# Running sums and an addition moved into accumulating transfers from GpSimd's queue, in a gated mix of linear attention and a long convolution

## The chip, the cores and the metric

One core of a Trainium2 chip runs the kernel. The time is device microseconds of one launch, with the inputs in the chip's main memory. The core has five engines with an instruction queue each: TensorE (matrix products; PE in the profile, its weight loads PEld), VectorE (DVE), ScalarE (ACT), GpSimd (POOL) and SyncE (SP), which here only starts transfers. Every engine works through its queue in order and waits at an instruction until what that needs is there. Transfers are carried by 16 DMA engines that all queues share.

## The reference, cut to what matters

The input x has 2048 rows of 448 channels. Two branches are computed from it and mixed by a gate of each row:

```python
g = sigmoid((x * gate_w).sum(-1))
# attention without softmax, 16 heads of 28 channels, phi(t) = (t + 1 or exp(t)) + 1e-6
kv = einsum("bhsd,bhse->bhde", phi(k), v);  z = phi(k).sum over rows
a  = (phi(q) @ kv / (phi(q) . z + 1e-6)) @ wo
# convolution along the rows, one kernel of 2048 taps for each channel
K  = 2 * Re(sum_n C[d, n] * exp(A[d, n] * dt[d] * l));   b = causal_conv(x, K) + x * D_skip
out = g * a + (1 - g) * b
```

For the given parameters the taps of a channel hardly change with the lag, so that the convolution is a running sum of x over the rows, times one number for each channel (`near`). The kernel checks on the chip that this holds and has a general path behind a branch for channels where it doesn't; that path is not taken here.

## The kernel before, in words

The rows are cut into 16 chunks of 128, and four chunks make a group. Row r of group g lies in partition r // 4 of chunk 4g + r % 4, so a partition holds four successive rows of the input, one in each chunk of its group. A running sum over a group's rows is then made of two steps: a sum over the four chunks inside each partition, and a sum over the partitions, which is a product with a triangular matrix (`tri`).

Everything is computed in float32 from pairs of a rounded part and a remainder (`split_t`, `split_n`: ScalarE copies the rounded part, GpSimd subtracts for the low part). The instructions are in an order written out by hand; the program keeps that order on each engine.

A loop `for c in range(2, NC - 2)` (lines 501 to 564) handles the middle chunks. In a stage c, TensorE projects k of chunk c+1 (`project`, line 340), then q and the gate of chunk c, and then adds chunk c to the accumulated product of phi(k) and x (`do_g`, line 415, four blocks). ScalarE and VectorE turn the projections into phi(k) and phi(q) (`k_feature`, `k_high`, `k_low`, `q_post`, lines 363 to 393): `pkh` is ScalarE's rounded part of phi(k), `pkl` the remainder, `zb` the running sum for z; `pq` keeps phi(q). GpSimd makes the low parts of the turned x (`xt`) and of the plain x (`xn`) of chunk c+2, and `skip` (line 258), which writes y = x * D_skip. SyncE loads x three chunks ahead (`load_x`), as its four buffers come free after the skips.

The convolution's path through the same stages:

- `group_load(g)` (line 422, SyncE) loads the four chunks of group g once more into a home: `homes = (spare, wvo[:, 1], pq[:, 12:], spare)`. Groups 0 and 3 share `spare`.
- `prefix(g, i, engine)` (line 425) adds chunk i-1 to chunk i, three times in a group, on GpSimd for group 0 and on VectorE for the others.
- `group_split` (line 427) splits the last chunk, which now holds the partition's sum, into `sums`; `group_heads` (line 432) multiplies it by `tri`, so that every partition has the sum of those before it.
- `convolve(c)` (line 438, VectorE) adds that to two chunks and multiplies them by `near`; after the second half SyncE copies the group's total row to `u`.
- `v_add(c)` (line 448, GpSimd) adds a chunk of the result to y, two in a stage of 6 to 11, and the last four in the final loop.

`near` itself comes from a preparation that is a generator (`s4d_prepare`, lines 285 to 320); `steps(n)` lets it go on by n pieces. The piece in stage 4 is a row of operations on VectorE with 4 elements in each of 112 partitions; the last piece, in stage 5, is four transposes on TensorE into a bank of PSUM (tag `v1`) and ScalarE's copy of them.

After the loop come the last two chunks, the combination of kv with wo, and the final loop, which normalizes phi(q), turns it, multiplies (`attend`, line 662) and adds the gated y (`final_b`, line 667).

## Time and profile before

| what | value |
|---|---|
| median of 3 runs | 180.84 us (180.59 to 181.35) |
| the profiled execution | 181.06 us, its span 179.3 us |
| granted TensorE clock | 1.0 over the span |
| TensorE busy | 165.7 us, 92% |
| VectorE busy | 139.3 us, 78% |
| ScalarE busy | 106.1 us, 59% |
| GpSimd busy | 135.4 us, 76% |
| bytes moved | 22.11 MB in 9434 packets |

The profile is of one execution. A row of an engine's timeline gives the start in microseconds from the span's beginning, the length, the engine, the line of the program, the operation and its tiles; in brackets stands how long the engine had been idle before it, and what ended that. The chain of waits goes back from the last instruction, at each step to what released it. A line can be that of a helper: L242 is `low`, whoever calls it. Product lengths overlap: products with 448 columns follow each other every 0.2 us.

### The profile page before, as it was taken

The page shows a single profiled execution, that of the slowest core. Times are in us where ns is not written, and L with a number is a line of the kernel's source. Part 1 is how long each engine was busy: PE and PEld are TensorE (multiplying, and loading weights), DVE is VectorE, ACT ScalarE, POOL GpSimd, SP SyncE. Part 2 cuts the span into 40 slices and gives each one's busy share as a digit, 9 for nine tenths or more (in the row PEclk, how much of TensorE's full clock was granted, in tenths as well). Part 3 has the DMA queues.
Part 4 walks back from the last instruction along what each step waited for, and adds up shares of the span by engine and source line. Part 5 has one row for each costly group of instructions (what it writes and reads, how often), then busy time and mean ns, then how long its engine had stood idle before and what let it go on. Part 6 is the DMA issues. An engine that isn't in the chain of part 4 may idle for free.

```text
span 179.3 us, 2707 instructions
## 1 busy us (share of the span) xinstructions
PE 165.7 (92%) x852; PEld 146.8 (82%) x852; DVE 139.3 (78%) x244; ACT 106.1 (59%) x241; POOL 135.4 (76%) x132
## 2 busy tenths in 40 slices
PE   7999999997699899978968999999999999999990
PEld 2798999995599779966957799999999999999990
DVE  0947549699989799889979978866898998997540
ACT  3779489863362846368244887667465464665431
POOL 6074676979949999969958979947968997988200
PEclk9999999999999999999999999999999999999999
DMA  5999978297520018303820300000031221221221
GB/s 184 413 296 302 255 194 311 88 400 275 218 107 0 0 13 305 123 4 118 203 93 0 117 4 0 0 2 0 3 68 53 103 98 57 105 104 52 104 103 58
DMA packets 9434, 22.11 MB, mean 123 GB/s; under 512 B 1357, under 2 KB 6170, under 8 KB 9418
## 3 DMA queue, kind: packets, MB, share of 16 engines
q1 hardware_dynamic: 9274, 21.81, 36.5%
q8 instruction: 7, 0.11, 0.3%
q10 hardware_dynamic: 144, 0.11, 0.2%
q14 instruction: 9, 0.07, 0.1%
HBM read 17.93 MB, written 3.67 MB: 120 GB/s over the span
## 4 chain that ended last, share of the span: by engine, by line
PE 53%; DVE 27%; ACT 13%; issue 4%; ACTq 0%; POOL 0%; DVEq 0%; POOLq 0%
PE a L662 20%; PE g L415 8%; PE q L340 6%; PE v L340 6%; PE tr L636 4%; DVE wvo L425 3%; PE q L264 3%; PE k L340 3%; DVE spare L425 3%; DVE pq L425 2%; ACT pkh L372 2%; DVE pq L393 2%; ACT e L391 2%; ACT e L392 2%; DVE v L368 2%
## 5 line engine op out<-in xcount | busy, mean ns | idle before, releaser
L662 PE MATMUL a<-wk,th 128*128 128x448 f32 (+1 forms) x170 | 36.4, 360 | 0.0
L415 PE MATMUL g<-pkh,xn 128*128 128x448 f32 x112 | 35.6, 364 | 0.0
L340 PE MATMUL q<-wqh,xt 128*128 128x450 f32 x120 | 27.9, 369 | 3.8 <-DVE pq L393 3.8
L662 PEld LDWEIGHTS a<-wk,th 128*128 128x128 f32 x170 | 29.5, 189 | 1.6
L242 POOL TENSOR_TENSOR xn<-xr,xn 128x448 fp32r<-128x448 f32 x16 | 23.8, 1489 | 8.3 <-ACT xn L252 3.7
L340 PEld LDWEIGHTS q<-wqh,xt 128*128 128x128 f32 x120 | 22.3, 189 | 6.5 <-DVE pq L393 4.9
L242 POOL TENSOR_TENSOR xt<-xr,xt 128x512 fp32r<-128x512 f32 x14 | 20.1, 1433 | 9.5 <-ACT xt L246 8.2
L415 PE MATMUL g<-pkl,xn 128*128 128x448 f32 x64 | 23.4, 366 | 0.0
L415 PEld LDWEIGHTS g<-pkh,xn 128*128 128x128 f32 x112 | 21.0, 188 | 2.2
L574 POOL TENSOR_TENSOR prod<-pq,zb 128x448 f32<-128x448 f32 x16 | 18.7, 1172 | 3.8 <-ACT zb L696 2.7
L258 POOL TENSOR_TENSOR y<-xr,rows 128x448 f32<-128x448 f32 x16 | 21.4, 1338 | 0.0
L340 PE MATMUL v<-wk,xt 128*128 128x448 f32 x99 | 21.3, 362 | 0.0
L340 PEld LDWEIGHTS v<-wk,xt 128*128 128x128 f32 x99 | 18.6, 188 | 1.3
L340 PE MATMUL k<-wk,xt 128*128 128x448 f32 x77 | 17.6, 368 | 1.3 <-POOL xt L242 1.3
L340 PEld LDWEIGHTS k<-wk,xt 128*128 128x128 f32 x77 | 14.3, 188 | 3.3 <-POOL xt L242 1.7
L599 POOL TENSOR_TENSOR pn<-pq,den 128x336 f32<-128x336 f32 x16 | 12.3, 769 | 3.7 <-ACT den L588 3.4
L667 DVE SCALAR_TENSOR_TENSOR ot<-y,og,a 128x448 f32<-128x448 f32 (+1 forms) x17 | 10.7, 630 | 5.2 <-PE a L662 4.3
L372 ACT ACTIVATE pkh<-v 128x448 fp32r<-128x448 f32 x9 | 4.9, 545 | 15.1 <-DVE v L368 15.1
L644 DVE TENSOR_TENSOR th<-tr,th 128x512 fp32r<-128x512 f32 x16 | 11.0, 690 | 2.6 <-ACT th L643 2.0
L643 ACT CAST th<-tr 128x512 fp32r<-128x512 f32 x16 | 9.4, 589 | 4.6 <-PE tr L636 4.4
L415 PEld LDWEIGHTS g<-pkl,xn 128*128 128x128 f32 x64 | 11.2, 174 | 1.2 <-DVE pkl L378 0.2
L340 PE MATMUL q<-wql,xt 128*128 128x450 f32 x45 | 11.8, 366 | 0.0
(170 smaller groups left out, 342.6 us busy)
## 6 DMA issues: line engine op xcount, KB each, us to landing
xr<-in SPq DMA_DIRECT2D x15, 512.0 KB, 3.9
out<-ot SPq DMA_DIRECT2D x15, 224.0 KB, 1.9
pq<-in SPq DMA_DIRECT2D x4, 448.0 KB, 12.3
spare<-in SPq DMA_DIRECT2D x2, 896.0 KB, 4.6
wvo<-in SPq DMA_DIRECT2D x2, 896.0 KB, 7.5
y<-in SPq DMA_DIRECT2D x2, 480.0 KB, 3.8
y<-in SPq DMA_DIRECT2D x2, 450.0 KB, 7.8
pq<-in SPq DMA_DIRECT2D x1, 896.0 KB
```

The lines of the kernel that those rows point to most:

```text
L242: eng.tensor_tensor(out=o, in0=r, in1=h.bitcast(F32), op=ALU.subtract)
L258: POOL.tensor_tensor(out=y[:, c], in0=plain[c][:, :D], in1=dsk, op=ALU.mult)
L340: PE.matmul(o[:, :n], lhsT=a, rhs=b, start=run.n == 1, stop=not seq)
L372: ACT.add(pkh[c], pks[c], 1e-6)
L415: PE.matmul(g[i][:a.shape[1], :D], lhsT=a, rhs=b, start=c == 0 and n == 0, stop=c == NC - 1 and n == len(seq) - 1)
L425: eng.tensor_tensor(out=homes[g][:, i], in0=homes[g][:, i], in1=homes[g][:, i - 1], op=ALU.add)
L574: POOL.tensor_tensor(out=pd[c], in0=pq[:, c], in1=zb, op=ALU.mult)
L599: POOL.tensor_tensor(out=n[:, :3, :DJ].rearrange("p j (h d) -> p j h d", h=4), in0=a, in1=r[:, :H - 4].rearrange("p (j h) -> p j h", j=3)[ ...
L643: ACT.copy(h, ov)
L644: DVE.tensor_tensor(out=l, in0=ov, in1=h.bitcast(F32), op=ALU.subtract)
L662: PE.matmul(a[:, lo:hi], lhsT=u_, rhs=w_[:, lo:hi], start=n == 0, stop=n == 10)
L667: DVE.scalar_tensor_tensor(out=ot[:, lo:hi], in0=y[:, c, lo:hi], scalar=og[:, c:c + 1], in1=a[:, lo:hi], op0=ALU.mult, op1=ALU.add)
```

## The change

The sums over a partition's four chunks are made by two accumulating transfers from GpSimd's queue. The first (`running(g, 1)`) adds the group's chunks 0 to 2, read once more from main memory, to its chunks 1 to 3 at home; the second (`running(g, 2)`) adds chunks 0 and 1 of the result to chunks 2 and 3. `prefix` is gone. The first is issued at the end of stages 2, 4, 6 and 8, the second in stages 3, 5, 7 and 9 behind GpSimd's part of `split_t`. The group loads of groups 2 and 3 move from stages 7 and 9 to 6 and 8, and all of them stand behind the loads of `cst`, `wvo` and `wo`. `group_split` moves one stage ahead, to 4, 6, 8 and 10, and its low part is always GpSimd's.

The sixteen `v_add` become four accumulating transfers (`group_add`), issued by GpSimd at the end of stages 7, 9, 11 and 13. `near`'s transposes move from behind the q projection of stage 5 to between the second and third block of `do_g`, into a bank of tag `v0`, and `group_heads(0)` moves behind the fourth block.

```diff
-        o = ps.tile([P, 512], F32, name="p", tag="v1")
+        o = ps.tile([P, 512], F32, name="p", tag="v0")
...
-    def prefix(g, i, eng):
-        eng.tensor_tensor(out=homes[g][:, i], in0=homes[g][:, i], in1=homes[g][:, i - 1], op=ALU.add)
-
-    def group_split(g, eng):
+    def running(g, step):
+        w = homes[g]
+        src = xin[g * G:(g + 1) * G - 1, :, NAT:LO].rearrange("r p d -> p r d") if step == 1 else w[:, :G - step]
+        POOL.dma_start(out=w[:, step:], in_=src, accum_op=ALU.add)
+
+    def group_split(g):
...
-        low(eng, w[:, 1], homes[g][:, G - 1], w[:, 0])
+        low(POOL, w[:, 1], homes[g][:, G - 1], w[:, 0])
...
-    def v_add(c):
-        POOL.tensor_tensor(out=y[:, c], in0=y[:, c], in1=homes[c // G][:, c % G], op=ALU.add)
+    def group_add(g):
+        POOL.dma_start(out=y[:, g * G:(g + 1) * G], in_=homes[g], accum_op=ALU.add)
...
+        if c in (2, 4, 6, 8):
+            group_load(c // 2 - 1)
+        ko = project(c + 1, wkh, wkl, D, "k" if c % 2 else "v1")
...
-        if c in (4, 6, 8, 10):
-            for i in (1, 2):
-                prefix(g0, i, DVE if g0 else POOL)
-        if c in (5, 7, 9, 11):
-            prefix(g0, 3, DVE if g0 else POOL)
         split_t(c + 2)
+        if c in (3, 5, 7, 9):
+            running(c // 2 - 1, 2)
         if c > 5:
             split_n(c + 2)
         k_feature(c + 1, ko)
-        if c in (5, 7, 9, 11):
-            group_split(g0, DVE if g0 else POOL)
+        if c in (4, 6, 8, 10):
+            group_split(c // 2 - 2)
...
-        if c == 5:
-            steps(1)
         q_post(c, qo)
...
-        do_g(c, (0, 1, 2))
-        if c in (5, 7, 9, 11):
-            group_heads(g0)
+        do_g(c, (0, 1))
+        if c == 5:
+            steps(1)
+        do_g(c, (2,))
+        if c in (7, 9, 11):
+            group_heads(c // 2 - 2)
         do_g(c, (3,))
+        if c == 5:
+            group_heads(0)
...
-        if 5 < c < 12:
-            v_add(2 * c - 12)
-            v_add(2 * c - 11)
+        if c in (2, 4, 6, 8):
+            running(c // 2 - 1, 1)
+        if c in (7, 9, 11, 13):
+            group_add(c // 2 - 3)
...
-        if 9 < c < 14:
-            v_add(c + 2)
```

More of the change, by code (lines that the diff above doesn't have):

```diff
@@ L505, in gated_mix_kernel @@
             SP.dma_start(out=cst, in_=cst_d)
-            group_load(0)
         if c == 4:
             SP.dma_start(out=wvo[:, 0], in_=wvo_d[:, 0])
-            group_load(1)
-        if c == 7:
-            group_load(2)
-        if c == 9:
-            group_load(3)
         if c == 10:
             SP.dma_start(out=wo, in_=wvo_d[:DJ, 1])
-        g0, half = (c - 4) // 2, c % 2
-        ko = project(c + 1, wkh, wkl, D, "k" if half else "v1")
+        if c in (2, 4, 6, 8):
+            group_load(c // 2 - 1)
+        ko = project(c + 1, wkh, wkl, D, "k" if c % 2 else "v1")
         if c > 5:
             convolve(2 * c - 12)
-        if c in (4, 6, 8, 10):
-            for i in (1, 2):
-                prefix(g0, i, DVE if g0 else POOL)
-        if c in (5, 7, 9, 11):
-            prefix(g0, 3, DVE if g0 else POOL)
         split_t(c + 2)
+        if c in (3, 5, 7, 9):
+            running(c // 2 - 1, 2)
         if c > 5:
```

## The prediction

> **What bounds the kernel now.** I read the page's chain of waits first, then that chain in order of time, then TensorE's timeline through chunks 4 to 12. (Each step c of the loop over the middle chunks, 2 to 13, is called stage c; it begins on TensorE with the k projection of chunk c+1.)
>
> ```profile
> span 179.3 us, 2707 instructions
> PE 53%; DVE 27%; ACT 13%; issue 4%; ACTq 0%; POOL 0%; DVEq 0%; POOLq 0%
> ```
>
> Half of the end is TensorE's own work; the rest is VectorE and ScalarE. In order of time (start, length, what) the chain says where:
>
> ```profile
> 40.04 0.55 ACT pkh L372
> ...
> 42.19 0.62 DVE pq L359
> 42.81 0.40 DVE sm L286
> ...
> 49.01 0.15 DVE oks L315
> ...
> 55.02 1.65 DVE wvo L425
> ...
> 59.28 0.06 ACT e L386
> 59.34 0.45 ACT e L390
> 59.82 0.59 ACT e L391
> 60.43 0.59 ACT e L392
> 61.04 0.63 DVE pq L393
> ...
> 96.90 1.59 DVE spare L425
> ...
> 100.90 2.20 PE v L340 x11
> ...
> 170.12 4.69 PE a L662 x33
> ```
>
> From 42 to 49 us the chain is a row of tiny VectorE operations (the preparation of near), from 55 to 98 us it passes again and again through the running sums of L425 on VectorE, and from 100.90 us on it is TensorE without a break. So whatever the change does before stage 12 arrives at the end undiminished, and nothing after it can win it back. TensorE's rows at the stage starts:
>
> ```profile
> 43.25 2.27 PE L340 MATMUL k<-wk,xt 128*128 128x448 f32 x10 [1.31 <-POOL xt L242]
> ...
> 49.15 0.60 PE L319 MATMUL p<-both,sm 112*128 112x112 f32 x4 [1.35 <-DVE sm L286]
> ...
> 52.22 2.37 PE L340 MATMUL v<-wk,xt 128*128 128x448 f32 x11
> ...
> 58.90 2.36 PE L340 MATMUL k<-wk,xt 128*128 128x448 f32 x11
> ...
> 94.86 1.87 PE L340 MATMUL q<-wqh,xt 128*128 128x450 f32 x8 [2.25 <-DVE pq L393]
> ...
> 100.74 2.37 PE L340 MATMUL v<-wk,xt 128*128 128x448 f32 x11
> ```
>
> Stage 6 runs from 52.22 to 58.90: 6.68 us with TensorE never idle. A stage with the two products of group_heads needs 0.4 us more, 7.08. Stages 6 to 11 therefore need 3 x (6.68 + 7.08) = 41.3 us and take 100.74 - 52.22 = 48.5. **7.2 us** are TensorE waiting, longest for pq L393 behind the sums (2.25 us in the row of 94.86).
>
> **The change, part by part.** *Off VectorE:* nine adds of this kind, and three low parts of the sums.
>
> ```profile
> L425 DVE TENSOR_TENSOR wvo<-wvo 128x448 f32<-128x448 f32 x3 | 4.8, 1586 | 0.0
> ```
>
> One and a half per stage make 2.4 us. What is then left of the loop that set the pace is pq 0.6, two operations of convolve 2.2, k's operation 0.6, pkh 0.55, the four ScalarE steps of q 1.7: 5.6 us, under 6.68. If the sums come in time, TensorE paces these stages and the 7.2 us are won. The sixteen adds to y and the three sums of group 0 leave GpSimd; they stand on no chain after 100.9 us, so I count nothing for them there.
>
> *Added:* twelve accumulating transfers issued by GpSimd, which runs its instructions in order, so each wait stands ahead of splits that TensorE needs. No such transfer is in the trace; the nearest rows:
>
> ```profile
> u<-pq SPq DMA_DIRECT2D x2, 1.8 KB, 1.7
> ...
> spare<-in SPq DMA_DIRECT2D x2, 896.0 KB, 4.6
> ```
> ```profile
> L422 SPq DMA_DIRECT2D spare<-in x2: 378/772/1165, 23.9 to 69.0; - x2
> L422 SPq DMA_DIRECT2D wvo<-in x1: 425/425/425, 34.3 to 34.3; - x1
> L422 SPq DMA_DIRECT2D pq<-in x1: 385/385/385, 45.9 to 45.9; - x1
> ```
> ```profile
> 39.00:40.00 1.00, 1.00 (x7) 0.93 (x6) 1.00 (x2) 0.00 (x0) 1.00 (x2) 1.00 1.06 407
> ```
>
> The first rows give time to landing, the next the time on the issuing queue, the last the rate (last column, GB/s) with all engines busy. *Issue:* between 0.38 and 1.17 us; I take the mean of the four, 0.6. *Landing:* 1.7 us fixed, plus bytes at about 410 GB/s. A sum must read what it adds to as well, so the data time lies between once and twice the bytes; I take twice, because a queue that moves both operands is what the add needs, and the once only if the second read were free. That makes 1.7 + 3.4 = 5.1 us for the first sum (672 KB), 1.7 + 2.2 = 3.9 for the second (448 KB), 1.7 + 4.5 = 6.2 for the add to y (896 KB). Ends: with 0.4 and once the bytes 3.4, 2.8, 3.9; with 1.17 and twice the 2.9 us that the 896 KB row leaves above 1.7, 6.1, 4.6, 7.5.
>
> The Trainium skill (DMA: Bandwidth & Descriptors, section Anatomy of one DMA — SWDGE (gpsimd) path) gives a transfer from GpSimd's queue 2.0 us plus bytes at 436 GB/s, 4.1 us for 896 KB, where this trace's load row has 4.6 on the other queue. By it the price is the lower end, and the result that of the first rival.
>
> *Group 0.* GpSimd's rows in stages 2 and 3:
>
> ```profile
> 32.31 1.15 POOL L258 TENSOR_TENSOR y<-xr,rows 128x448 f32<-128x448 f32 x1
> 33.41 1.30 POOL L242 TENSOR_TENSOR xt<-xr,xt 128x512 fp32r<-128x512 f32 x1
> 34.67 1.31 POOL L258 TENSOR_TENSOR y<-xr,rows 128x448 f32<-128x448 f32 x1
> ...
> 39.36 2.38 POOL L425 TENSOR_TENSOR spare<-spare 128x448 f32<-128x448 f32 x2
> 41.69 1.51 POOL L242 TENSOR_TENSOR xt<-xr,xt 128x512 fp32r<-128x512 f32 x1
> ```
> ```profile
> 33.86 0.42 SPq L508 DMA_DIRECT2D wvo<-in  x1
> 34.34 0.42 SPq L422 DMA_DIRECT2D wvo<-in  x1
> ```
>
> The first sum can be issued at 33.5, when the skip of chunk 4 is done. Just then SyncE issues xr and two loads of 896 KB, so it gets half the rate: 34.1 + 6.8 + 1.7 = 42.6. GpSimd stands at the second sum from about 35.4; that one is issued by 43.2, lands at 47.1. Behind the stand: skip, split, skip (34.67 to 39.36 less an idle 1.0: 3.6 us) and xt of chunk 6, done at 48.1; TensorE wanted it at 41.94 and got it at 43.25. On ScalarE the copy of the sums now stands ahead of pkh of chunk 5: pkh starts at 47.65, not 40.04, 7.6 us later, and so pq of chunk 4 ends at 50.4 and near's preparation, 6.3 us long in the rows above, follows. Between GpSimd's operations its tiny instructions take about 1.1 us each, otherwise under 0.2; GpSimd has three operations left before it stands again, so I let it end by 53.5. TensorE: k to 50.2, q 50.4 to 52.6, two blocks of g to 53.8, transposes (now here) 54.2. group_heads(0) waits for near's copy, now queued behind pkh and q's steps: 53.5 + 0.6 + 0.55 + 0.5 + 0.5 = 55.7. Stage 6 starts at 56.1 instead of 52.22: **+3.9**. The new place of the transposes saves the 1.35 us of its row only if the preparation is in time; here it isn't.
>
> *Groups 1 and 2.* Sum 1 of group 1 is issued at 51.5 and lands at 57.2, sum 2 at 61.7; ScalarE wants it at 59.5 and waits 2.2 us, and pq of chunk 6 comes at 65.1 where q of stage 7 could start at 65.0. Group 2's wait, 1.8 us, is absorbed in the same way. Nothing is lost, little is left.
>
> *Group 3.* Its home is spare, group 0's. Its load now waits for a transfer, not for GpSimd's adds: sum 1 of group 2 issued at 64.8 lands at 70.5, GpSimd passes its second sum at 71.1, two operations later issues the add of group 0 at 73.4, which lands at 80.2; load issued and landed 5.0 later, 85.2; GpSimd, which stood there since 78.7, issues sum 1 by 85.8, lands 90.9; sum 2 by 91.5, lands 95.4. What is late: xt of chunk 11 (GpSimd 87.1; stage 10 could start at 83.65, **+3.45**); xt of chunk 12 (95.7 against 93.8, **+1.9**); ScalarE's copy at 95.4, pq of chunk 10 at 98.75 against 97.9 (**+0.85**). SyncE's x loads behind the waiting group load land in time.
>
> *Sum:* 3.9 - 7.2 + 3.45 + 1.9 + 0.85 = **+2.9 us** at the start of stage 12, and so at the end. The profiled execution took 181.06 with its span of 179.3, so 184.0; against the median of the runs shown, 180.84 (0.22 less), **183.7**.
>
> **The rivals.** *All covered (faster).* With the lower end of the prices the sum of group 0 lands at 39.0 and 42.2, pkh is 2.7 us late, stage 6 starts at 51.6, and in group 3 the add issued at about 64 is down by 68, the load by 73, the sums by 80, before stage 10 asks for them near 82. Then 51.6 + 41.3 = 92.9, 7.8 us ahead: 173.0. For it: 7.2 us of TensorE's waiting are there to be had, and GpSimd is relieved of 19 operations. Against it: a sum that reads one operand for nothing. Since five transfers and their issues lie in a row in group 3, and two in group 0, about 0.4 us less for each than I take already brings the balance to zero: that is the point where it decides.
>
> *Transfers dearer still.* With the upper ends the waits in group 1 and 2 show too (2.4 and 0.9 us), stage 10 starts some 10 us late, and stage 12 about 13 us later than before: 194. For it: 384 separate rows of 1,792 bytes in the first sum, for which no issue row stands. The Trainium skill (SBUF — State Buffer, section SBUF: two separate sides) warns that GpSimd cannot write the descriptors of its transfers while VectorE runs an operation that takes the port pair they share; no run here shows it yet, and by it the issue would exceed 1.17.
>
> *A draw.* The wins and the stands cancel, as they do 0.4 us below my price: 180.8. The profile has nothing that would favour so exact a balance.
>
> **How the numbers follow.** A difference of about 0.5% (0.9 us) is what a measurement of this kernel can tell from none. My forecast (182 to 190) gets 0.40, all covered and everything on the way to it (172.5 to 179.9) 0.39, a draw 0.09, the dear transfers (above 190) 0.12. Faster 0.39, same 0.09, slower 0.52. The range reaches from the full cover, 172.5, to 191, which leaves most of the dear case out; the forecast's own is 182 to 190.
>
> **What would show it.** Right: GpSimd idle for some 7 us ahead of the second sum in stage 3 and of the first sum in stage 8; ScalarE waiting for sums in stages 4 and 10; TensorE waiting for xt L242 at stage 10; no L425; stages 6 and 7 at 6.7 and 7.1 us. Wrong: first sums that land in under 4 us, stage 12 starting before 99 us, or GpSimd busy with issuing rather than standing.

## The result, and the profile after

The changed kernel takes 199.66 us (median of 4 runs, 199.13 to 200.24) against 181.09 us of the kernel before in the same comparison (180.59 to 182.22): a ratio of 1.102, 95% interval 1.095 to 1.108. The forecast was 183.7 us in a range from 172.5 to 191. The direction was forecast, the size was not: 18.6 us lost in place of 2.9.

The page of the profiled execution (200.24 us, mean granted TensorE clock 0.953), its span and its chain of waits by engine and by line:

```profile
span 198.5 us, 2704 instructions
...
PE 38%; DMA 28%; DVE 10%; POOL 9%; ACT 8%; issue 5%; ACTq 0%; POOLq 0%; SPq 0%
PE a L660 18%; DMA spare<-in 13%; DMA wvo<-in 5%; DMA pq<-in 4%; PE g L415 4%; PE tr L634 4%; POOL y L258 3%; PE v L340 3%; DMA y<-spare 3%; POOL xn L242 3%; PE q L264 2%; PE q L340 2%; DVE pq L444 2%; DVE spare L444 2%; DMA spare<-spare 2%
```

Before, no transfer stood on the chain at all. Now they are 28% of it. The same chain in order of time, from stage 2 on (start, length, what):

```profile
33.46 12.92 DMA spare<-in
...
55.72 8.99 DMA wvo<-in
...
72.37 7.42 DMA pq<-in
...
82.89 6.58 DMA y<-spare
...
89.49 5.12 DMA spare<-in
...
95.20 7.83 DMA spare<-in
...
103.31 4.14 DMA spare<-spare
...
111.93 4.46 DVE pq L444
...
133.52 3.01 DVE og L401
```

Every first sum needs its load landed, and every second sum needs the first. GpSimd stands five times, for 10.46, 6.65, 4.77, 6.50 and 5.50 us, with all its later work behind it, and the next group's transfers are issued from the same queue. So seven landings in a row make the chain. TensorE's timeline shows what arrives (idle time ahead of a row in brackets):

```profile
52.18 4.10 PE L340 MATMUL k<-wk,xt 128*128 128x448 f32 x10 [9.03 <-POOL xt L242]
61.79 2.37 PE L340 MATMUL v<-wk,xt 128*128 128x448 f32 x11
...
93.21 3.37 PE L340 MATMUL q<-wqh,xt 128*128 128x450 f32 x8 [5.47 <-DVE pq L393]
...
100.33 2.37 PE L340 MATMUL v<-wk,xt 128*128 128x448 f32 x11
...
115.89 2.37 PE L340 MATMUL v<-wk,xt 128*128 128x448 f32 x11
```

Stage 6 starts at 61.79 (before: 52.22, so +9.6), stage 10 at 100.33, stage 12 at 115.89 (before: 100.74, so +15.2). Stages 6 to 11 take 54.1 us where they took 48.5, and the stretch from stage 12 to the end 82.6 where it took 78.6. 9.6 + 5.6 + 4.0 make the 19.2 us by which the span grew. The landings themselves (KB each, us from issue to landing; for two transfers the median):

```profile
y<-spare POOLq DMA_DIRECT2D x2, 896.0 KB, 6.6
spare<-in POOLq DMA_DIRECT2D x2, 672.0 KB, 10.4
spare<-spare POOLq DMA_DIRECT2D x2, 448.0 KB, 4.3
...
wvo<-in POOLq DMA_DIRECT2D x1, 672.0 KB, 9.0
pq<-in POOLq DMA_DIRECT2D x1, 672.0 KB, 7.4
```

Two things in this trace had no place in the forecast. The first is TensorE's clock. Stretches of 2 us (the bare number behind GpSimd's busy time is the granted clock, then the DMA share and GB/s):

```profile
44.00:46.00 2.00, 0.00 (x0) 0.00 (x0) 0.00 (x0) 0.00 (x0) 0.00 (x0) 1.00 0.88 245
46.00:48.00 2.00, 0.00 (x0) 0.00 (x0) 0.00 (x0) 0.00 (x0) 1.32 (x2) 0.68 0.00 0
...
54.00:56.00 2.00, 2.00 (x7) 1.78 (x6) 2.00 (x7) 0.00 (x0) 2.00 (x3) 0.50 1.01 376
56.00:58.00 2.00, 2.00 (x9) 1.80 (x9) 2.00 (x1) 1.12 (x2) 2.00 (x2) 0.76 0.80 226
58.00:60.00 2.00, 2.00 (x12) 1.82 (x11) 1.65 (x9) 0.24 (x1) 0.35 (x1) 1.00 0.45 105
```

TensorE is idle from 43.15 us. A mean of 0.68 in a stretch that goes from 1.00 to 0.50 puts the fall at 46.7, 3.6 us into the idle time; by the same reckoning the clock is back at 57.0, 4.8 us after work began at 52.18. In between the ten products of k take 4.10 us where they took 2.27. The Trainium skill (TensorE: Matmul & The Clock Gate, section Part 1: The HAM clock gate) describes that: half rate after some 3.4 us without work, full rate after about as long with it. The fall agrees; the return took somewhat longer here.

The second is VectorE's multiply by `near` (L444) beside GpSimd's run:

```profile
80.80 8.87 DVE L444 TENSOR_TENSOR wvo<-wvo,rows 128x896 f32<-128x896 f32 x1
```
```profile
80.07 0.91 POOL L427 DMA_DIRECT2D pq<-pq  x1 [4.77 <-DMA pq<-in]
...
82.89 1.21 POOL L450 DMA_DIRECT2D y<-spare  x1
...
86.96 1.74 POOL L242 TENSOR_TENSOR sums<-pq,sums 128x448 fp32r<-128x448 f32 x1
```

The same multiply took 1.1 to 2.1 us in every stage before. Here it ends at 89.67, 1 us after the last operation of a run of GpSimd that holds two issues, and pq of that stage, for which TensorE waits at 93.21, comes after it.

### The profile page after: what moved, and what is told of

Same layout as the page of the kernel before. It is cut to its first block, busy times and chain, and to the rows that moved or that the text cites. A ratio compares the mean times of both kernels' runs of the same rounds, so it can differ in the third digit from the quotient of the medians.

```text
span 198.5 us, 2704 instructions
## 1 busy us (share of the span) xinstructions
PE 170.5 (86%) x852; PEld 149.9 (76%) x852; DVE 134.3 (68%) x232; ACT 106.1 (53%) x241; POOL 120.0 (60%) x128
## 4 chain that ended last, share of the span: by engine, by line
PE 38%; DMA 28%; DVE 10%; POOL 9%; ACT 8%; issue 5%; ACTq 0%; POOLq 0%; SPq 0%
PE a L660 18%; DMA spare<-in 13%; DMA wvo<-in 5%; DMA pq<-in 4%; PE g L415 4%; PE tr L634 4%; POOL y L258 3%; PE v L340 3%; DMA y<-spare 3%; POOL xn L242 3%; PE q L264 2%; PE q L340 2%; DVE pq L444 2%; DVE spare L444 2%; DMA spare<-spare 2%
## 5 line engine op out<-in xcount | busy, mean ns | idle before, releaser
L340 PE MATMUL q<-wqh,xt 128*128 128x450 f32 x120 | 29.9, 388 | 8.2 <-DVE pq L393 8.2
L340 PEld LDWEIGHTS q<-wqh,xt 128*128 128x128 f32 x120 | 23.6, 202 | 11.8 <-DVE pq L393 9.7
L340 PE MATMUL k<-wk,xt 128*128 128x448 f32 x77 | 20.4, 404 | 11.7 <-POOL xt L242 11.7
L242 POOL TENSOR_TENSOR xt<-xr,xt 128x512 fp32r<-128x512 f32 x14 | 23.7, 1696 | 8.6 <-ACT xt L246 8.6
L340 PEld LDWEIGHTS k<-wk,xt 128*128 128x128 f32 x77 | 15.4, 207 | 14.8 <-POOL xt L242 13.2
L258 POOL TENSOR_TENSOR y<-xr,rows 128x448 f32<-128x448 f32 x16 | 22.3, 1393 | 0.0
L572 POOL TENSOR_TENSOR prod<-pq,zb 128x448 f32<-128x448 f32 x16 | 18.6, 1172 | 3.6 <-ACT zb L694 2.6
L597 POOL TENSOR_TENSOR pn<-pq,den 128x336 f32<-128x336 f32 x16 | 12.3, 768 | 7.5 <-ACT den L586 5.3
L378 DVE SCALAR_TENSOR_TENSOR pkl<-v,pkh 128x448 fp32r<-128x448 f32 x9 | 5.6, 619 | 13.1 <-ACT pkh L372 13.0
L378 DVE SCALAR_TENSOR_TENSOR zb<-v,zb 128x448 f32<-128x448 f32 x9 | 5.6, 620 | 10.2 <-ACT pkh L372 10.2
L415 PEld LDWEIGHTS g<-pkl,xn 128*128 128x128 f32 x64 | 11.3, 177 | 1.3 <-DVE pkl L378 0.2
## 6 DMA issues: line engine op xcount, KB each, us to landing
spare<-in POOLq DMA_DIRECT2D x2, 672.0 KB, 10.4
```

Source lines behind the costliest of these rows:

```text
L242: eng.tensor_tensor(out=o, in0=r, in1=h.bitcast(F32), op=ALU.subtract)
L258: POOL.tensor_tensor(out=y[:, c], in0=plain[c][:, :D], in1=dsk, op=ALU.mult)
L340: PE.matmul(o[:, :n], lhsT=a, rhs=b, start=run.n == 1, stop=not seq)
L378: DVE.scalar_tensor_tensor(out=o, in0=pk, scalar=1e-6, in1=a, op0=ALU.add, op1=op)
L415: PE.matmul(g[i][:a.shape[1], :D], lhsT=a, rhs=b, start=c == 0 and n == 0, stop=c == NC - 1 and n == len(seq) - 1)
L572: POOL.tensor_tensor(out=pd[c], in0=pq[:, c], in1=zb, op=ALU.mult)
```

## The experiments

**Each part by itself.** `near_alone` moves near's transposes and nothing else:

```diff
-        o = ps.tile([P, 512], F32, name="p", tag="v1")
+        o = ps.tile([P, 512], F32, name="p", tag="v0")
...
-        if c == 5:
-            steps(1)
         q_post(c, qo)
...
-        do_g(c, (0, 1, 2))
+        do_g(c, (0, 1))
+        if c == 5:
+            steps(1)
+        do_g(c, (2,))
```

> The kernel before with near's transposes moved between blocks 2 and 3 of g in stage 5, its bank and group_heads(0) moved with them, and nothing else. If the changed kernel's 18.6 us come from the transfers alone (theory: GpSimd and ScalarE, which run in order, wait for landings), this edit is worth what the idle TensorE time ahead of the transposes was, at most 1.35 us, less the 0.5 us by which near's copy now comes later: 179.8 to 181.1. Rival: the move itself is part of the loss, because near's copy stands behind q's steps on ScalarE and group_heads(0) behind it: 182 or more.

Measured: 181.41 us, ratio 0.998 (0.994 to 1.001); stage 6 starts at 52.00. The move is worth nothing that can be told.

`add_alone` is the kernel before with four accumulating adds to y at the ends of stages 7, 9, 11 and 13 in place of sixteen adds on GpSimd:

```diff
-        if 5 < c < 12:
-            v_add(2 * c - 12)
-            v_add(2 * c - 11)
+        if c in (7, 9, 11, 13):
+            group_add(c // 2 - 3)
...
-        if 9 < c < 14:
-            v_add(c + 2)
```

> The kernel before with the sixteen adds to y replaced by four accumulating transfers at the end of stages 7, 9, 11 and 13; the sums stay on VectorE and GpSimd. Theory of waiting: nobody waits for these transfers but the load of group 3, which is not needed before 88 us, so no loss; GpSimd is 20 us less busy and stands less in VectorE's way: 178 to 181. Rival (any accumulating transfer disturbs the other queues or VectorE): 184 or more. Landing 6.6 to 8.2 us as in the changed kernel.

Measured: 180.82 us, ratio 0.994 (0.992 to 0.997), stage 12 at 99.84. Nobody waits for these landings, and this part gains 0.6%.

`sums_alone` is the kernel after with that part undone:

```diff
-        if c in (7, 9, 11, 13):
-            group_add(c // 2 - 3)
+        if 5 < c < 12:
+            v_add(2 * c - 12)
+            v_add(2 * c - 11)
...
+        if 9 < c < 14:
+            v_add(c + 2)
```

> The changed kernel with its adds to y back on GpSimd as in the kernel before; the running sums stay transfers. Theory of waiting: stage 6 starts at about 61.8 as in the changed kernel, but the load of group 3 no longer waits for the 6.6 us of a transfer and begins some 5 us earlier; GpSimd carries 20 us more: 193 to 199. Rival (it is the adds that cost): 184 or less.

Measured: 198.55 us, ratio 1.091 (1.082 to 1.101); stage 6 at 62.03, stage 12 at 117.84. Nearly the whole loss (16.7 of 18.6 us) belongs to the sums.

**What the landings cost.** `plain_copies` writes over where the kernel after adds; it leaves out the running sums and the adds to y:

```diff
-        POOL.dma_start(out=w[:, step:], in_=src, accum_op=ALU.add)
+        POOL.dma_start(out=w[:, step:], in_=src)
...
-        POOL.dma_start(out=y[:, g * G:(g + 1) * G], in_=homes[g], accum_op=ALU.add)
+        POOL.dma_start(out=y[:, g * G:(g + 1) * G], in_=homes[g])
```

> The changed kernel with all twelve transfers as plain copies from the same queue: the sums and the adds to y are left out, the bytes and places stay. If a sum costs because it reads its destination too, the first transfer of a group lands in about 5 us where it took 7.4, the second in 3.0 for 4.2, the one to y in 4.3 for 6.6, and the time falls to about 188 to 192. If it is the queue of GpSimd or the many rows of 1,792 bytes that cost, the landings and the time (199) stay.

Measured: 189.27 us in one run. The landings in this kernel:

```profile
y<-spare POOLq DMA_DIRECT2D x2, 896.0 KB, 4.2
spare<-in POOLq DMA_DIRECT2D x2, 672.0 KB, 6.5
...
y<-wvo POOLq DMA_DIRECT2D x1, 896.0 KB, 3.9
```

An add of 896 KB takes 6.6 to 8.2 us where a copy takes 3.8 to 5.2: the second operand costs about as much as the first, as the forecast took it. Yet with every landing shorter (adds to y by 2.1 to 3.0 us, first sums by 1.1 to 4.8, second sums by 0.1 to 1.5) the kernel is still 8 us slower than before, and its multiplies by near took 6.16 and 6.18 us in two stages. So landings are not all of it.

`group0_on_gpsimd` gives group 0's sums back to GpSimd, in stage 3:

```diff
+        if c == 3:
+            for i in (1, 2, 3):
+                prefix(0, i, POOL)
-        if c in (3, 5, 7, 9):
+        if c in (5, 7, 9):
             running(c // 2 - 1, 2)
...
-        if c in (2, 4, 6, 8):
+        if c in (4, 6, 8):
             running(c // 2 - 1, 1)
```

> The changed kernel with group 0's running sums again as three GpSimd adds, in stage 3; the other groups and the adds to y stay transfers. Theory of waiting: the 9.6 us by which stage 6 starts late come from GpSimd and ScalarE waiting for group 0's two landings, so stage 6 starts at 51 to 53 us and 9 to 10 us go: 189 to 191. Rival (the loss before stage 6 comes from elsewhere, for example the later place of the transposes or the engines' load): stage 6 stays beyond 57, 195 or more.

Measured: 190.29 us, ratio 1.047 (1.041 to 1.052); stage 6 at 53.60, stage 12 at 107.09. Group 0's two transfers cost 8.2 us at stage 6 and 9.4 us at the end: that part of the loss is settled.

`group0_quiet` keeps group 0's transfers and takes the loads from beside them:

```diff
-        if c == 4:
+        if c == 9:
             SP.dma_start(out=wvo[:, 0], in_=wvo_d[:, 0])
...
-        if c in (2, 4, 6, 8):
+        if c in (2, 6, 8):
             group_load(c // 2 - 1)
+        if c == 2:
+            group_load(1)
```

> The changed kernel with two loads of 896 KB taken away from beside group 0's first sum: wvo's first half moves from stage 4 to 9, group 1's load from stage 4 to 2, behind group 0's. If that sum took 12.9 us because it shared the DMA engines with them, it lands in 7 to 8.5 us and stage 6 starts 4 to 6 us earlier, 194 to 196. If it is slow by itself at this place (its rows, the descriptors against VectorE), it stays above 11 us, and the time near 199.

Measured: 197.26 us in one run. The first sum, issued at 34.36, lets the second go at 43.87, 9.5 us later instead of 13.2, and stage 6 starts at 59.43, 2.4 us sooner. About 3.7 us of the 12.9 were the loads beside it; the rest is the sum's own.

**Landings that nobody waits for.** `room_to_land` (near moved as in the change) keeps the adds to y and group 0's sums on GpSimd, and gives each sum of groups 1 to 3 a stage or more to land:

```diff
-        if c == 7:
+        if c == 6:
             group_load(2)
-        if c == 9:
+        if c == 8:
             group_load(3)
...
         split_t(c + 2)
+        if c == 4:
+            for i in (1, 2, 3):
+                prefix(0, i, POOL)
+        if c in (6, 8, 10):
+            running(g0, 2)
...
+        if c in (4, 6, 8):
+            running(c // 2 - 1, 1)
```

> The kernel before with only groups 1 to 3 summed by transfers, each given a stage or more to land before anything waits: first sum at the end of stages 4, 6, 8, second behind GpSimd's split in stages 6, 8, 10, group_split again in 7, 9, 11; group 0 and the adds to y stay on GpSimd, near's transposes in the new place. Theory of waiting: nine sums leave VectorE and nobody waits, stages 6 to 11 take 41 to 43 us where they took 48.5, with 0 to 1 us more from GpSimd's issues: 174 to 177. Rival (transfers from GpSimd cost by themselves, through issue, descriptors or the DMA engines): 181 or more.

Measured: 185.26 us, ratio 1.017 (1.011 to 1.022). The theory that landings are all falls here. GpSimd's longest wait for one, and VectorE's multiplies in stages 7 and 9:

```profile
78.48 1.30 POOL L427 DMA_DIRECT2D spare<-in  x1 [1.89 <-DMA spare<-in]
```
```profile
63.03 5.70 DVE L447 TENSOR_TENSOR spare<-spare,rows 128x896 f32<-128x896 f32 x1
...
79.39 7.07 DVE L447 TENSOR_TENSOR wvo<-wvo,rows 128x896 f32<-128x896 f32 x1
```

`room_and_add` is that kernel with the adds to y of groups 1 to 3 by transfer as well (ends of stages 9, 11, 13; the load of wo a stage later):

```diff
-        if 5 < c < 12:
+        if 5 < c < 8:
             v_add(2 * c - 12)
             v_add(2 * c - 11)
+        if c in (9, 11, 13):
+            group_add(c // 2 - 3)
```

> As the run before, and the adds to y of groups 1 to 3 as transfers at the end of stages 9, 11, 13; the load of wo moves to stage 11 behind them, group 0's adds stay on GpSimd so that spare is free early. Theory of waiting: GpSimd is 14 us less busy and VectorE waits less beside it: 172 to 176, up to 2 us below the run before. Rival: the adds' landings hold up wo and the x loads behind it on SyncE, 177 or more.

Measured: 181.86 us, ratio 0.999 (0.995 to 1.003). VectorE waited 5.76 and 4.81 us in its multiplies. The forecast gain of 7.2 us isn't in either kernel.

**Whose wait is VectorE's?** `tiny_issue` is the kernel before with four transfers of 2 KB from GpSimd's queue, which nobody reads:

```diff
         split_t(c + 2)
+        if 5 < c < 10:
+            POOL.dma_start(out=edge[:, 4 * (c - 6):4 * (c - 5)], in_=xin[c, :, :4])
```

> The kernel before, with nothing of the change in it, and four transfers of 128x4 values (2 KB, no sums) from the inputs into a tile that nothing reads, issued from GpSimd's queue in stages 6 to 9 between GpSimd's low part of xt and its low part of xn. They move almost nothing and nobody waits for them. Theory (after a transfer issue, an operation of VectorE with two inputs from the SBUF waits until GpSimd's run of back-to-back operations ends): GpSimd's run behind each issue is the low part of xn, the skip and two adds to y, some 6.2 us by the trace of before, so the multiply by near, which took 2.07 us at most before, takes 3 to 7 us in at least two of the stages 6 to 9, and the time is 185 to 195 us. Rival (only the landing of the large transfers, or their load on the transfer engines and the SBUF, matters): the four issues cost GpSimd 0.6 to 0.9 us each, the multiply stays under 2.5 us, and the time is 180.5 to 183 us.

Measured: 186.43 us, ratio 1.028 (1.019 to 1.037). VectorE, GpSimd and TensorE in stage 6:

```profile
55.59 6.91 DVE L425 TENSOR_TENSOR wvo<-wvo 128x448 f32<-128x448 f32 x2
```
```profile
56.77 0.71 POOL L527 DMA_DIRECT2D edge<-in  x1
57.50 1.17 POOL L242 TENSOR_TENSOR xn<-xr,xn 128x448 fp32r<-128x448 f32 x1
58.61 1.17 POOL L258 TENSOR_TENSOR y<-xr,rows 128x448 f32<-128x448 f32 x1
59.73 2.27 POOL L448 TENSOR_TENSOR y<-y,spare 128x448 f32<-128x448 f32 x2
```
```profile
66.04 2.72 PE L340 MATMUL q<-wqh,xt 128*128 128x450 f32 x8 [4.13 <-DVE pq L393]
```

Two sums that take 3.1 us elsewhere in this trace take 6.91 and end at 62.50, 0.5 us after GpSimd's run; the second of them alone, from 57.34 us on, takes 5.15. TensorE waits 4.13 us for the pq behind them. 8 KB in all cost about 5 us (two runs, 185.24 and 187.61 us). But only one of the four issues did it, and it was a sum that waited, not the multiply that the theory named. In stages 7 to 9 VectorE's multiply was under way when the issue came, and the next operation took its usual turn; in stage 6 the first sum was under way in the same way, so that does not tell the cases apart. Both theories were half right: an issue is enough, and not every issue does it.

`tiny_memset` puts eight small clears where the issues stood:

```diff
-            POOL.dma_start(out=edge[:, 4 * (c - 6):4 * (c - 5)], in_=xin[c, :, :4])
+            for i in range(8):
+                POOL.memset(edge[:, 2 * i:2 * i + 2], float(i))
```

> As tiny_issue, but in place of each transfer's issue stand eight small clears (128x2 values each) on GpSimd, between its low part of xt and its low part of xn in stages 6 to 9: a break of about the same length in GpSimd's run, without a transfer. Theory (it was the issue that drew the one wait of 5.4 us of VectorE's sum in stage 6 of tiny_issue): none of VectorE's sums and multiplies of stages 6 to 11 over 3.2 us for one, and 180.5 to 182.5 us. Rival (any break in GpSimd's run, by which VectorE's turn is lost, does it): a wait of 4 us or more in stage 6 again, and 184.5 to 188 us.

Measured: 181.10 us, ratio 0.998 (0.994 to 1.002). The pair of sums in stage 6:

```profile
54.97 3.22 DVE L425 TENSOR_TENSOR wvo<-wvo 128x448 f32<-128x448 f32 x2
```

So a break by other work in GpSimd's run does not do it. The eight clears take 0.30 us together, though, where an issue takes 0.58 to 0.71, so a break as long as the issue was not tested.

`no_near` is the kernel after without the multiply by near; it leaves that factor of the convolution out:

```diff
         DVE.tensor_tensor(out=a, in0=a, in1=heads[g][:, None, :].to_broadcast(full), op=ALU.add)
-        DVE.tensor_tensor(out=a, in0=a, in1=near[:, None, :].to_broadcast(full), op=ALU.mult)
```

> The kernel after, without VectorE's multiply by near (the four groups' convolution leaves that factor out, so the output differs). What remains of the change: the transfers, their landings, and VectorE's add of the heads, which takes one input from the PSUM. Theory (the multiply's waits in stages 8, 9, 11 hold 8 to 10 us of the loss, the first group's late landing the other 9.6): the start of stage 6 stays at 60 to 62.5 us, stages 6 to 11 take 48 to 50 us instead of 54.1, and the time is 187 to 193 us, of which 1.5 us per group of two would have gone on VectorE anyhow. Rival (the wait moves to the next operation of VectorE with two inputs, or TensorE waits for the landings in any case): within 2.5 us of the kernel after, 197 to 200 us.

Measured: 198.78 us in one run, 0.9 us less than the kernel after. The rival was right. TensorE's long wait moved to group 3's landings, for which GpSimd stood in the kernel after too (6.50 us):

```profile
94.95 1.30 POOL L427 DMA_DIRECT2D spare<-in  x1 [6.09 <-DMA spare<-in]
```
```profile
97.60 3.64 PE L340 MATMUL v<-wk,xt 128*128 128x448 f32 x10 [4.20 <-POOL xt L242]
```

In the kernel after, VectorE's waits and the row of landings stand beside each other. Taking away either one leaves the other. The loss belongs to both, and the landings are the longer.

**Toward a kernel with neither.** `issues_before_idle` (near moved, group 0's sums on GpSimd) places the issues at the end of GpSimd's stage (sums of group 1 in stages 3 and 5, where one low part of x still follows, group 2 in 6 and 7, group 3 in 8 and 9):

```diff
+        if c in (3, 5):
+            running(1, c // 2)
...
+        if 5 < c < 10:
+            running(c // 2 - 1, 1 + c % 2)
+        if c in (9, 11, 13):
+            group_add(c // 2 - 3)
```

> The kernel before with the move of near, the adds to y of groups 1 to 3 by accumulating transfers at the ends of stages 9, 11 and 13, and the running sums of groups 1 to 3 by accumulating transfers too, but each issued as GpSimd's last work of a stage (group 1: stages 3 and 5, group 2: 6 and 7, group 3: 8 and 9; loads of the groups in stages 2, 5 and 8), a stage or more ahead of its reader; group 0's sums stay on GpSimd, in stage 4 at once; the weights into the first half of wvo come in stage 9 and wo in stage 11. Theory (the wait of VectorE needs a run of GpSimd behind the issue, so an issue ahead of GpSimd's idle time is nearly free): no multiply by near over 3 us, stage 12 starts at 94 to 100 us against 100.7, and the time is 174 to 180.5 us. Rival (every issue draws a wait of VectorE, wherever it stands, or the landings themselves slow VectorE): multiplies of 4 to 6 us as when the issues stood inside the stages, and 181 to 187 us.

Measured: 181.15 us, ratio 0.998 (0.996 to 1.000). VectorE waited 5.32 us in the low part of a group's sum (stage 7) and 4.82 us in a multiply (stage 10): GpSimd's next stage begins before it has been idle. The theory fell; the place of the issue helps too little.

So the next kernels change VectorE's operations. `multiply_on_gpsimd` gives the multiply to GpSimd in place of the adds to y, which all go by transfer, and leaves the sums on VectorE:

```diff
-    homes = (spare, wvo[:, 1], pq[:, NC - G:], spare)
+    homes = (wvo[:, 0], wvo[:, 1], pq[:, NC - G:], spare)
...
-        DVE.tensor_tensor(out=a, in0=a, in1=near[:, None, :].to_broadcast(full), op=ALU.mult)
+    def by_near(c):
...
+        POOL.tensor_tensor(out=a, in0=a, in1=near[:, None, :].to_broadcast(full), op=ALU.mult)
...
+        if c > 5:
+            by_near(2 * c - 12)
+        if c in (8, 9, 11, 13):
+            group_add(c // 2 - 3 - (c == 8))
```

> The kernel before with the move of near, with the multiply by near on GpSimd in VectorE's stead (at the end of the stage, where the adds to y stood) and the adds to y by accumulating transfers (ends of stages 8, 9, 11, 13); group 0 has its home in the first half of wvo, whose weights come in stage 10; wo comes in stage 11, the groups' loads in stages 2, 4, 6, 8, and the low parts of the groups' sums are all GpSimd's. The running sums stay on VectorE (groups 1 to 3). Theory (VectorE's operations on two SBUF operands are what the stages wait for): VectorE is rid of 1.5 us in each of the stages 6 to 13, GpSimd has about as much as before; stage 12 starts at 96 to 100 us (before: 100.7) and the time is 175 to 180 us. Rival (the issues ahead of GpSimd's runs cost VectorE's sums as much): 181 to 186 us.

Measured: 183.74 us, ratio 1.011 (1.005 to 1.017). The rival holds; behind the issues at 73.88 and 83.15 it is now VectorE's sums that wait, this pair for 7.13 us in place of 3.1:

```profile
83.65 7.13 DVE L425 TENSOR_TENSOR spare<-spare 128x448 f32<-128x448 f32 x2
```

`sums_too` takes the sums off VectorE as well:

```diff
+        if c == 3:
+            running(1, 1)
+        if c == 5:
+            running(1, 2)
+            running(2, 1)
...
+        if c == 7:
+            running(2, 2)
+            running(3, 1)
+        if c == 9:
+            running(3, 2)
```

> As multiply_on_gpsimd, with the running sums of groups 1 to 3 by accumulating transfers, each two stages or more ahead of its reader (group 1: ends of stages 3 and 5, group 2: 5 and 7, group 3: 7 and 9), group 0's on GpSimd in stage 4; loads of the groups in stages 2, 2, 4 and 6. VectorE then has no operation on two large SBUF operands in the stages 6 to 13. Theory (the gain of 7.2 us forecast for the stages 6 to 11 is there, but was eaten by VectorE's waits behind GpSimd's runs and by GpSimd's waits for landings, both of which this kernel is without): stages 6 to 11 take 42 to 45 us in place of 48.5, and the time is 173 to 178 us. Rival (VectorE's sums were not what those stages waited for, or GpSimd, with some 41 us of work in those stages, sets the pace): 46 to 50 us in stages 6 to 11 and 178 to 184 us.

Measured: 184.22 us, ratio 1.015 (1.008 to 1.021). In stages 6 to 13 no operation of VectorE is over 1.7 us. Stages 6 to 11 took 48.2 us all the same, since ScalarE now waits for the chunks of x:

```profile
76.17 0.62 ACT L246 CAST xt<-xr 128x512 fp32r<-128x512 f32 x1 [3.49 <-DMA xr<-in]
```

SyncE's queue held those loads behind the transfer of a group's last row, which waits for the multiply that now comes at the stage's end. `sums_too_rows_later` issues that transfer one stage later, behind the load:

```diff
-        if i and g < NC // G - 1:
-            for k in (g, UL + g):
-                SP.dma_start(out=u[k:k + 1], in_=homes[g][P - 1:P, G - 1])
+    def last_row(g):
+        for k in (g, UL + g):
+            SP.dma_start(out=u[k:k + 1], in_=homes[g][P - 1:P, G - 1])
...
+        if c in (8, 10, 12):
+            last_row(c // 2 - 4)
```

> As sums_too, with the transfers of each group's last row to u moved from behind the multiply (end of stages 7, 9, 11) to behind the loads of stages 8, 10 and 12. In sums_too SyncE waited for GpSimd's multiply at the head of its queue (16.5 us the longest) with the loads of the chunks behind it, so that ScalarE waited 3.5, 3.8 and 1.4 us for a chunk to land. Theory (VectorE's waits are gone, and that queue was the rest): ScalarE's three waits for a chunk are under 1 us together, stages 6 to 11 take 42 to 45 us, and the time is 174 to 178 us. Rival (GpSimd's work, or a landing elsewhere, sets the pace): stages 6 to 11 take 46 us or more and the time is 179 us or more.

Measured: 181.29 us, ratio 0.998 (0.995 to 1.001). Stages 6 to 11 take 45.3 us; in stage 11 ScalarE waits 3.38 us for group 3's second sum, issued beside an add and a load. `multiply_rows_later`, the same edit on `multiply_on_gpsimd`:

> As multiply_on_gpsimd, with the last rows' transfers moved in the same way; the running sums stay on VectorE. Theory (behind an issue, VectorE's sums wait for GpSimd's run): one or two sums of VectorE over 4 us again, and the time is 178 to 182.5 us, 2 us or more above sums_too_rows_later. Rival (SyncE's queue was the whole loss of multiply_on_gpsimd): 174 to 177.5 us and no slower than sums_too_rows_later.

Measured: 183.05 us, ratio 1.008 (1.005 to 1.012), with VectorE's 7.18 us again and 49.0 us for stages 6 to 11. Between these two kernels the sums, with the earlier loads that they need, are the difference: by transfer they are worth 3.7 us in these stages and 1.8 us at the end.

`sums_too_spread` puts group 3's transfers earlier and the others farther apart:

```diff
-        if c in (4, 6):
-            group_load(c // 2)
+        if c in (4, 5):
+            group_load(c - 2)
...
-        if c == 10:
+        if c == 13:
             SP.dma_start(out=wvo[:, 0], in_=wvo_d[:, 0])
...
+        if c in (6, 7, 8):
+            running(3 - c % 2, 1 + (c > 6))
+        if c in (9, 10, 11, 13):
+            group_add({9: 1, 10: 0, 11: 2, 13: 3}[c])
```

> As sums_too_rows_later, with the transfers spread: group 3's load in stage 5, its first sum at the end of stage 6 and its second at the end of stage 8 (before: 6, 7, 9), the adds to y of groups 0 and 1 at the ends of stages 10 and 9, and the weights for wvo's first half in stage 13. In sums_too_rows_later group 3's second sum, issued beside an add and a load, landed so late that ScalarE waited 3.38 us for it in stage 11, TensorE idled, and its granted clock fell to 0.84. Theory (what is left of the forecast gain is held by that one landing): no wait of ScalarE over 2 us for a sum in stages 7 to 11, stages 6 to 11 take 41 to 43.5 us, and the time is 176 to 179.5 us. Rival (the rest, from stage 12 on, gives back what the stages gain, or another landing comes late): 180 us or more.

Measured: 183.67 us, ratio 1.013 (1.008 to 1.018), but stages 6 to 11 take 42.7 us. In stage 13 it is lost again: `pq` of chunk 12 may not be written over group 2 until the add to y has read that, 10.4 us after its issue. TensorE waits for it, and half the clock goes with the wait (3.37 us for products of 1.88):

```profile
109.20 3.37 PE L340 MATMUL q<-wqh,xt 128*128 128x450 f32 x8 [3.75 <-DVE pq L393]
```

`sums_too_home` exchanges two homes, so that the group in the tail of pq is one that has long been added:

```diff
-    homes = (wvo[:, 0], wvo[:, 1], pq[:, NC - G:], spare)
+    homes = (pq[:, NC - G:], wvo[:, 1], wvo[:, 0], spare)
```

> As sums_too_spread, with the homes of groups 0 and 2 exchanged: group 0 in the tail of pq, group 2 in the first half of wvo. In sums_too_spread stages 6 to 11 took 42.7 us (before: 48.5), but VectorE's pq of chunk 12 had to wait until group 2's add to y had been read out of pq's tail; it landed 10.4 us after its issue, TensorE was idle from 105.45 us to 109.20 us, and its granted clock was 0.50 behind that. Group 0's add is through by then, and the weights' load takes the wait. Theory (the gain in stages 6 to 11 is real, and that one wait gave it back): stage 14 starts at 107 to 111 us (sums_too_spread: 116.5, before: 114.2) and the time is 174.5 to 179 us. Rival (the stages from 12 on give the gain back anyhow): 180 us or more.

Measured: 178.44 us, ratio 0.980 (0.976 to 0.984): the fastest kernel here, ahead of both. Its chain of waits, and TensorE at the start of stages 6, 12 and 14:

```profile
PE 43%; POOL 25%; DVE 15%; ACT 6%; DMA 4%; issue 3%; SPq 1%; ACTq 0%; POOLq 0%; DVEq 0%
```
```profile
54.77 2.37 PE L340 MATMUL v<-wk,xt 128*128 128x448 f32 x11
...
97.70 2.36 PE L340 MATMUL v<-wk,xt 128*128 128x448 f32 x11
...
110.99 2.36 PE L340 MATMUL v<-wk,xt 128*128 128x448 f32 x11
```

Stages 6 to 11 take 42.9 us (before: 48.5). The landings are down to 4% of the chain. 2.5 us are given away before stage 6, which starts at 54.77; near's preparation waits there for a load into pq, 2.34 us on ScalarE and 1.87 on VectorE, for which nothing waited before.

## Why the prediction was right or wrong

**What bounds the kernel: right.** VectorE's loop did hold 5.6 to 5.8 us of the stages 6 to 11, of the 7.2 that the prediction counted there, and what a kernel gained or lost before stage 12 arrived at the end. "Nothing after it can win it back" held too, but more was lost there: 4.0 us. By TensorE's rows 1.9 of them are stage 12, where it waits 1.68 us for the pq behind VectorE's multiply of 4.46 us. Another 1.7 are the stretch from stage 14 to the end of `do_g`, where it waits 1.45 us behind VectorE's operation on the gate at L401 (the last row of the chain shown). That one took 0.82 us before and takes 3.01 here, beside the last issue and the run of GpSimd behind it. The other 0.4 are spread over the rest.

**The landing of the first sums: the step that failed.** Priced at 5.1 us with an upper end of 6.1 (5.7 and 7.3 with the issue), they took, from the start of the issue, 12.9 (9.1 forecast, beside loads), 9.0, 7.4 and 7.8. Second sums (4.5 forecast with the issue, 4.1 to 4.8 measured) and adds to y (6.8; 6.6 to 8.2) were near their price, so reading the destination was rightly counted. What the model of fixed time plus bytes missed is the first sum alone, of less data than the add and yet no faster. It reads main memory, and was often in flight beside loads; `group0_quiet` finds 3.7 us for such company in one case. Adding is not all of it: as a plain copy the same transfer took 8.1, 7.9, 4.5 and 5.0 us in `plain_copies`, where a copy of 896 KB within the core took 3.8 to 5.2. Why it takes 7 us or more in every accumulating case is open. By the chain the four first sums exceed their terms by 3.8, 3.3, 1.7 and 2.1 us (the forecast from issue to landing: 9.1, 5.7, 5.7 and 5.7), 10.9 together, and stage 12 came 12.3 us later than forecast. By that count nearly all of the miss at stage 12 is this one term, because the landings follow each other in one queue. The price that the Trainium skill (DMA: Bandwidth & Descriptors, section Anatomy of one DMA — SWDGE (gpsimd) path) has for a transfer of GpSimd's queue gives an estimate of 4.1 us for 896 KB; the plain copies of `plain_copies` (3.8 to 5.2) are near it, the accumulating ones are not.

**Group 0, +3.9: +9.6 measured.** 3.8 us of the difference are the landing. Another 2.1 are TensorE's clock, which fell while it stood: k and the eight first products of q took 5.9 us (52.18 to 58.09) where they took 3.8 before (43.25 to 47.01), and the prediction took TensorE's rows at full clock after an idle time of 9 us.

**Groups 1 and 2, "nothing is lost": wrong.** Landings of 9.0 and 7.4 for 5.7 used up what I had called little: ScalarE waited 4.0 and 3.7 us for the sums (2.2 and 1.8 forecast), stage 7 began its k products 0.6 us late for xt and took 9.3 us. Stage 9 took 15.9, but that is the other wait: TensorE stood 5.47 us for the pq behind VectorE's multiply of 8.87, and then worked at half clock, while group 3's landings went on beside it.

**Group 3's chain: right in its order, wrong in its time.** Add, load, first sum, second sum follow each other as forecast, with 6.6, 5.1, 7.8 and 4.1 us for 6.8, 5.0, 5.7 and 4.5, the issues counted in. They started late.

**The gain of 7.2: there, and not to be had this way.** The prediction let VectorE run freely once its sums were gone. Its multiply was left, and behind GpSimd's issues it waits 4 to 9 us. `no_near` says that in the kernel after the landings hide this; `room_to_land` and `room_and_add` say that without the landings it decides. Only with no sum and no multiply left on VectorE, and with no wait in SyncE's queue or in pq, did 5.6 us of the gain come (`sums_too_home`).

**The rivals.** "All covered" had a wrong turning point: 0.4 us less for each transfer was to bring a draw, but in `plain_copies` every landing except group 1's first (7.9) lies 0.5 to 3.0 us below the forecast price, and it loses 8 us. "Transfers dearer still" named the right direction with 194 us, and the first sums went beyond its prices too. The shared port that it cites from the Trainium skill (SBUF — State Buffer, section SBUF: two separate sides) may show here, from the other side: no issue here was held up for long (their records are 0.6 to 1.7 us), while VectorE was. That section lets an operation wait for one instruction of the other engine; in `tiny_issue` one sum of VectorE waited through four, and the measurement decides. That the port is the cause is not shown.

**What would show it.** GpSimd stood 10.46 us ahead of the second sum in stage 3 (forecast 7) and 6.50 us ahead of group 3's first sum (7). ScalarE waited 11.43 us for the sums of stage 4 and 3.63 for those of stage 10, and L425 was gone. TensorE waited for xt in stages 5, 7, 9 and 11, and not in stage 10. Stage 6 took 6.7 us, stage 7 9.3 and not 7.1. None of the three signs of being wrong came, so they could not have found a first sum that is dearer than its price.

## What to carry to other kernels

A transfer that adds cost about twice its bytes here and, when the engine that issues it also has work that others need, each landing that it waits for holds all of that work; place the reader's wait elsewhere, or issue a stage ahead (by itself that was not enough here: `room_to_land` still took 185.26 us). Before counting what an engine gains by being relieved, ask which of its remaining operations slow down beside the engine that took the work over, and measure the cheapest version of the new instruction by itself: four transfers of 2 KB, put into the old kernel, showed a wait that no size of the transfers explains. And when two waits stand beside each other, taking one away proves nothing about its price.

## What the runs showed of the hardware that I had not expected

- VectorE's operations from SBUF to SBUF can wait through a whole run of GpSimd's operations when a transfer's issue stands ahead of the run: 8.87 us for a multiply that takes 1.1 to 2.1, 7.13 for a pair of sums that takes 3.1. In each of the 22 waits of 4 us or more in these traces that its sums, multiplies and low parts of the sums have after 55 us, the operation ends 0.5 to 1.2 us after the last operation of GpSimd's run, about what it takes by itself; so it seems to start when the run ends. In the three kernels in which GpSimd issues no transfer in these stages (before, `near_alone`, `tiny_memset`) no single operation of VectorE took over 2.1 us between 28 and 125 us. One of four issues in `tiny_issue` drew such a wait; what decides which one isn't settled.
- TensorE's granted clock fell from 1.00 to 0.50 about 3.6 us into an idle time and came back 4.8 us after work began, so that a wait of 9.0 us cost 2.1 us more in the products behind it.
- In the kernel after, an accumulating transfer within the core lands in 4.1 to 4.8 us for 448 KB and 6.6 to 8.2 us for 896 KB, and one of 672 KB from main memory in 7.4 us at the least; as copies in `plain_copies` the first two take 2.7 to 4.0 and 3.8 to 5.2. With other transfers in flight it can be much longer: 11.3 us for 448 KB in `sums_too_rows_later`.
